# Two places where weights are split, one order inside the w_out units, and a last unit in three PSUM tiles

## The chip, the cores and the metric

The kernel runs on one core of a Trainium2 chip. The metric is the device time of one execution in microseconds (us). The kernel before took 1111.39 us, the median of three runs (1110.79 to 1111.77).

## The reference

Sigmoid attention, then a gated two-layer product, all in float32. With B = 8 batches, H = 12 heads, S = 448 positions and D = 64:

```
scores = q @ k.T / sqrt(64) - log(448)
attn   = 1 / (1 + exp(-scores))
x      = (attn @ v), heads side by side: 3584 x 768
h      = x @ w_in                      # 768 x 2048
g      = h * clip(h + 3, 0, 6) / 6
out    = g @ w_out                     # 2048 x 768
```

w_in and w_out arrive as 64-bit floats, which the kernel takes apart itself into 32-bit ones (`decode`: one ScalarE instruction and six VectorE ones for each piece).

## The kernel before

The engines are TensorE (PE), VectorE (DVE), ScalarE (ACT), GpSimd (POOL) and SyncE (SP), which issues every transfer. Each engine works through its instructions in the order in which the code was written (`manual_schedule`), so the order is set by hand: lists of steps (`on`), slots (`at_slot`) and units (`at_unit`) say in which step a piece of side work is written down.

Three stages follow each other on PE.

Attention has 168 steps. Step s writes the scores of step s, a sigmoid (`a`, L194), then the side work listed for s, then the product with v of step s - 2 (`av`). A finished pair is copied by ACT (`y`, L219) and added by DVE (`xr`, L220), which frees one of two PSUM buffers. Side work is the decoding of w_in, and for the first pair of batches four sums of x (`x_sums`, L234 to L240) and seven splits (`x_split`). A split turns a float32 tile into a high and a low part for PE: ACT casts (L69), DVE subtracts (L71).

The product stage, x times w_in, has 112 slots of 18 matmuls each (L345), seven products (M1 to M7) of Strassen's kind for each quarter. Slot n loads the weights of slot n + 5 into one of three staging buffers, casts those of slot n + 3 and subtracts those of n + 2; the subtraction frees the buffer. The first two w_out tiles (`w2_load`, `w2_split` for M1, h = 0 and 1) go through the same three buffers, in slots 90 to 97. A buffer is handed on in the order in which the code frees it.

The w_out stage has 56 units of 36 matmuls (L630): seven phases (M1, M2, M6, M7, M5, M4, M3), in each four pairs p, for each two halves h. Unit n needs `gx` of n, the split of a tile g of 128 x 1792, and the three w_out tiles of its phase and half. In unit n the code loads g of n + 4 (`g_load`), in two phases a second part of n + 3 (`g_load2`), sums the parts of n + 2 (`g_sum`) and splits g of n + 2. Between the cast and the subtraction of that split stands the unit's listed work (`plan`): decoding w_out pieces (`w2_unit`, L50 to L63), four sums of its quarters (`w2_sums`, three on DVE, L531 to L533, the fourth on POOL, L534), storing them (`w2_store`, L539), loading and splitting the next phase's tiles (L458, L69, L71). Two units make one PSUM tile `po` of three banks, which `post2` turns into a sum kept (`s`) or an output (`o`, L567); the last unit does it for its three parts one after another (L567, and the transfers of L594). A w_out tile with h = 1 can be cast only when PE is done with the unit before the phase, since its three buffers are all in use.

Of the kernel before, what the change touches and what calls it, by code (L numbers as in the profile page):

```python
# [8 lines left out]
F32 = mybir.dt.float32  # L9
# [7 lines left out]
B, H, S, D = 8, 12, 448, 64  # L17
DM, DF = 768, 2048
P = 128
# [5 lines left out]
EC = DM // P // 2  # L25
# [12 lines left out]
M1, M2, M3, M4, M5, M6, M7 = range(7)  # L38
A11, A12, A21, A22, S1, S2, S3, S4 = range(8)
# [27 lines left out]
def split(nc, hi, lo, a):  # L67

    nc.scalar.copy(hi, a)  # L69
    yield  # L70
    nc.vector.tensor_tensor(out=lo, in0=a, in1=hi.bitcast(F32), op=ALU.subtract)  # L71
    yield
# [20 lines left out]
def tile_kernel(ctx: ExitStack, tc: tile.TileContext, qk, vP, wi, wo, outT):  # L93
# [45 lines left out]
    def ring(name, shape, dtype):  # L139
        return dw.tile(shape, dtype, tag="ring", name=name, bufs=5)  # L140
# [10 lines left out]
    events, later, plan = {}, {}, {}  # L151
# [4 lines left out]
    def at_slot(n, f, *a):  # L156
        later.setdefault(n, []).append((f, a))

    def at_unit(n, f, *a):
        plan.setdefault(n, []).append((f, a))  # L160

    def over(when, steps, gen):
        for n in steps:
            when(n, next, gen, None)
# [78 lines left out]
    def x_split(p, k):  # L243
        x = xt[k].tile([P, 2, KC, S], F32R, tag="x", name=f"x_{p}_{k}")
        xts[p, k] = x
        yield from split(nc, x[:, 0], x[:, 1], xr[p].pop(k))
# [19 lines left out]
    def w2_unit(k, h, ec, held):  # L266

        st = staging(f"wo_{k}_{h}_{ec}", [P, FC * P, 2], I32)
        nc.sync.dma_start(out=st, in_=wo[k, h, :, ec * FC * P : (ec + 1) * FC * P])
        yield  # L270
        if ec == 0:
            held[k, h] = ring(f"w2_{k}_{h}", [P, EC, FC * P], F32)
        yield from decode(nc, st, held[k, h][:, ec])
        if ec == EC - 1 and k in (A11, A12):
            yield
            yield
            nc.sync.dma_start(out=dw2[k, h], in_=held.pop((k, h)))
# [5 lines left out]
    for u in range(4 * EC):  # L283
        kh, ec = divmod(u, EC)
# [19 lines left out]
    end0 = 2 * LB + LAG  # L304
    over(on, range(end0 + 1, end0 + 5), x_sums(nc.vector, 0))
    for i, k in enumerate((B11, B22, B21, T3, T1, T2, T4)):
        over(on, (end0 + 6 + 2 * i, end0 + 7 + 2 * i), x_split(0, k))
    for n in range(LA):
        on(NS - 10 + n, w1_load, n)
        over(on, (NS - 3 + n, NS - 2 + n), w1_split(n))  # L310
# [112 lines left out]
    units = [(i, p, h) for i in PHASES for p in range(NPR) for h in range(2)]  # L423
# [7 lines left out]
    def g_load(n):  # L431
        if n < len(units):
            i, p, h = units[n]
            first, _ = PARTS.get(MOVING[i], (MOVING[i], None))
            gr[n] = gset[n % 3].tile([P, FC, S], F32, tag="gr", name=f"gr_{n}")
            nc.sync.dma_start(out=gr[n], in_=gd[p, first, h])

    def g_load2(n):
        if n < len(units) and MOVING[units[n][0]] in PARTS:
            i, p, h = units[n]  # L440
            gs[n] = [ring(f"gr_{n}_{k}", [P, 2, S], F32) for k in range(2)]
            for k in range(2):
                nc.sync.dma_start(out=gs[n][k], in_=gd[p, PARTS[MOVING[i]][1], h][:, 2 * k : 2 * k + 2])

    def g_sum(n):
        for k, o in enumerate(gs.pop(n, ())):
            part = gr[n][:, 2 * k : 2 * k + 2]
            nc.vector.tensor_tensor(out=part, in0=part, in1=o, op=ALU.subtract)  # L448

    def g_split(n):  # L450
        gx[n] = gset[n % 3].tile([P, 2, FC, S], F32R, tag="gx", name=f"gx_{n}")
        yield from split(nc, gx[n][:, 0], gx[n][:, 1], gr.pop(n))
# [7 lines left out]
    def w2_split(i, h):  # L460
        st, gens = w2s.pop((i, h)), []
        for ec in range(EC):
            w = xs.tile(
                [P, 2, FC, P], F32R, tag="xT" if h else "xraw", name=f"w2_{i}_{h}_{ec}", bufs=3 if h else 5
            )
            flat = w.rearrange("p t c e -> p t (c e)")
            w2[i, h, ec] = w
            gens.append(split(nc, flat[:, 0], flat[:, 1], st[:, ec]))
        for _ in range(2):
            for g in gens:  # L470
                next(g)
            yield
# [12 lines left out]
    end = len(seq)  # L485
    for n in range(LA, end):
        over(at_slot, (n - LA, n - LA + 1), w1_split(n))
    for h in range(2):
        at_slot(end - 22 + h, w2_load, M1, h)
        over(at_slot, (end - 18 + 2 * h, end - 17 + 2 * h), w2_split(M1, h))  # L490

    def xt_close(*ks):
        for k in ks:
# [12 lines left out]
    for n, (i, q) in enumerate(seq):  # L506
# [10 lines left out]
    po_pool = ctx.enter_context(  # L517
        tc.tile_pool(name="ps_o", bufs=2, space=bass.MemoryType.PSUM, reuse_waits="tile")
    )
# [21 lines left out]
    def w2_direct(i, h):  # L541
        w2s[i, h] = made[h].pop(WEIGHT[i])

    for h, n in ((0, 0), (1, 9)):
        for e in range(2 * EC):
            k, ec = divmod(e, EC)
            u = n + e
            over(at_unit, [max(0, u - 1), u, u + 1, u + 1, u + 1, u + 1], w2_unit(A21 + k, h, ec, held))
        at_unit(n + 4, w2_reload, h)
        at_unit(n + 2 * EC + (h == 0), w2_sums, h)  # L550
        at_unit(n + 2 * EC + 2, w2_store, h, *((S1, A22, S3, S2) if h == 0 else (S1, A22, S3)))
        at_unit(n + 2 * EC + 3, w2_store, h, S4)
    for k, i in enumerate(PHASES[1:]):
        n = 8 * (k + 1)
        for h in range(2):
# [7 lines left out]
    po, so = {}, {}  # L563
    SIXTH = 1.0 / 6.0

    def stt(out, ps_in, other):
        nc.vector.scalar_tensor_tensor(out=out, in0=ps_in, scalar=SIXTH, in1=other, op0=ALU.mult, op1=ALU.add)  # L567
# [4 lines left out]
    def out_tile(i, p):  # L572
        return acc_ctx[0].tile([P, EC, S], F32, tag="o", name=f"o_{i}_{p}", bufs=2)

    def kept(i, p):
        return acc_ctx[0].tile([P, EC, S], F32, tag="s", name=f"s_{i}_{p}", bufs=2 * NPR)

    def post2(i, p, n):
        t = po.pop(p)[:, :, :S]
        if i == M1:  # L580
            so[p] = kept(i, p)
            nc.scalar.mul(so[p], t, SIXTH)
        elif i == M6:
            stt(so[p], t, so[p])
        elif i == M7:
            so["u3", p] = kept(i, p)
            stt(so["u3", p], t, so[p])
        else:
            eh, k, other = {M2: (0, 0, p), M5: (1, 1, ("u3", p)), M4: (1, 0, ("u3", p)), M3: (0, 1, p)}[i]
            o = out_tile(i, p)  # L590
            if n == len(units) - 1:
                for ec in range(EC):
                    stt(o[:, ec], t[:, ec], so[other][:, ec])
                    nc.sync.dma_start(out=outT[2 * p + k, eh * EC + ec], in_=o[:, ec])  # L594
                return
            stt(o, t, so[other])
            if i == M5:
                stt(so[p], t, so[p])
            at_unit(n + 1, put, p, eh, k, o)

    for n, (i, p, h) in enumerate(units):
        if n == 0:
            for _ in range(2):
                for f, a in later.pop(min(later)):
                    f(*a)
        elif n == 1:
            while later:
                for f, a in later.pop(min(later)):
                    f(*a)
            tmp_ctx.close()  # L610
            acc_ctx.append(ctx.enter_context(tc.tile_pool(name="acc", bufs=1, side="right", reuse_waits="tile")))
        g_load(n + 4)
        g_load2(n + 3)
        low = None
        if n + 2 < len(units):
            g_sum(n + 2)
            low = g_split(n + 2)
            next(low)
        for f, a in plan.pop(n, []):
            f(*a)  # L620
        if low is not None:
            next(low)
        if h == 0:
            po[p] = po_pool.tile([P, EC, 512], F32, tag="po", name=f"po_{i}_{p}")
        x = gx.pop(n)
        for ec in range(EC):
            w = w2[i, h, ec]
            for c in range(FC):
                for wk, xk in ((0, 0), (0, 1), (1, 0)):
                    nc.tensor.matmul(  # L630
                        po[p][:, ec, :S],
                        w[:, wk, c],
                        x[:, xk, c],
                        start=h == 0 and c == 0 and xk == 0 and wk == 0,
                        stop=h == 1 and c == FC - 1 and wk == 1,
                    )
        if h == 1:
            post2(i, p, n)
# [34 lines left out]
```

## Time and profile before

| | us |
|---|---|
| median of three runs | 1111.39 |
| the profiled execution | 1116.47 |
| its span | 1114.7 |
| PE busy | 1091.8 |
| attention, first matmul to the first product matmul | 4.4 to 263.7 |
| product stage | 263.7 to 687.2 |
| w_out stage | 687.2 to 1110.1 |

A row of the timeline has the start in us from the span's start, the duration, the engine, the line, the operation with out<-in, and in brackets the idle time before it and what ended it. "x18" says that the row merges 18 instructions. "SPq" rows are transfers being issued, not their landing. The chain of waits merges instructions the same way: start, length, engine, tile, line. A wait is given as engine and tile <- what it waited for: us in total, times, longest.

### The profile page before, as it was taken

To read this page: it belongs to the slowest core of one execution; us is meant where nothing else is said; L and a number is where in the kernel's file an instruction comes from. 1 tells how busy PE (TensorE), PEld (TensorE's weight loads), DVE (VectorE), ACT (ScalarE), POOL (GpSimd) and SP (SyncE) were. 2 spreads that over 40 slices of the span, in tenths; PEclk is the share of its full clock that TensorE was granted. 3 is DMA by queue.
4 is the path that set the end of the run, shared out by engine and by line. 5 is a ranking of instruction groups with operands and counts; after the bars stand their busy time and mean duration, and the time that the engine had idled before them with its cause. 6 is when DMAs were issued, how large, how long until landed. Compare 5 with 4: busy or idle time off the path is not lost.

```text
span 1114.7 us, 16569 instructions
## 1 busy us (share of the span) xinstructions
PE 1091.8 (98%) x6720; PEld 865.4 (78%) x6720; DVE 744.0 (67%) x710; ACT 560.7 (50%) x612; POOL 177.2 (16%) x84
## 2 busy tenths in 40 slices
PE   8999999999999999999999899999999999989998
PEld 3333633336999999999999799999889999979997
DVE  3579747644677986898687456887863447776541
ACT  6889888876446554644565444443322212222320
POOL 0214120000252352244121112110000000000000
PEclk9999999999999999999999899999999999999999
DMA  8876998966665886687666687959775357889641
GB/s 313 303 285 250 360 356 317 309 238 206 208 220 179 295 269 204 200 288 237 200 198 223 220 257 239 338 191 393 268 270 189 132 194 260 291 298 314 238 143 50
DMA packets 81484, 277.13 MB, mean 249 GB/s; under 512 B 7936, under 2 KB 22272, under 8 KB 81408
## 3 DMA queue, kind: packets, MB, share of 16 engines
q1 hardware_dynamic: 81408, 276.07, 71.2%
q8 instruction: 53, 0.87, 0.3%
q14 instruction: 23, 0.19, 0.0%
HBM read 189.92 MB, written 86.11 MB: 248 GB/s over the span
## 4 chain that ended last, share of the span: by engine, by line
PE 84%; DVE 9%; ACT 3%; DMA 3%; issue 2%; SPq 0%; DVEq 0%; ACTq 0%
PE po L630 28%; PE A L345 21%; PE D L345 10%; PE sc L192 10%; PE pv L209 10%; PE B L345 5%; DVE gr L448 2%; ACT gx L69 2%; DVE gx L71 1%; DVE w L71 1%; DMA ws<-dw 1%; DVE x L71 1%; DMA w2s<-dw 1%; DVE o L567 1%; ACT w L69 0%
## 5 line engine op out<-in xcount | busy, mean ns | idle before, releaser
L630 PE MATMUL po<-gx,w 128*128 128x448 f32 x2016 | 416.9, 369 | 6.0 <-ACT w L69 3.4
L630 PEld LDWEIGHTS po<-gx,w 128*128 128x128 f32 x2016 | 379.4, 188 | 43.3 <-ACT w L69 4.2
L345 PE MATMUL A<-x,w 128*128 128x448 f32 x1152 | 245.7, 371 | 4.9 <-ACT u L370 4.8
L345 PEld LDWEIGHTS A<-x,w 128*128 128x128 f32 x1152 | 218.2, 190 | 27.7 <-ACT u L370 5.7
L69 ACT CAST gx<-gr 128x1792 fp32r<-128x1792 f32 x56 | 94.7, 1694 | 238.6 <-PE po L630 137.0
L192 PE MATMUL sc<-qk 64*64 64x448 f32 x1344 | 191.5, 542 | 5.0 <-DMA qk<-qk 4.4
L209 PE MATMUL pv<-a,v 64*64 64x448 f32 x1344 | 190.4, 537 | 2.3 <-DVE xr L220 2.0
L194 ACT ACTIVATE a<-sc,bias_s 128x896 f32<-128x896 f32 x168 | 169.0, 1010 | 46.5 <-PE sc L192 43.5
L71 DVE TENSOR_TENSOR w<-ws,w 128x768 fp32r<-128x768 f32 x112 | 154.1, 1385 | 32.2 <-ACT w L69 31.9
L71 DVE TENSOR_TENSOR gx<-gr,gx 128x1792 fp32r<-128x1792 f32 x56 | 113.2, 2022 | 70.5 <-ACT gx L69 70.5
L192 PEld LDWEIGHTS sc<-qk 64*64 64x64 f32 x1344 | 63.9, 134 | 80.5 <-issue 62.9
L209 PEld LDWEIGHTS pv<-a,v 64*64 64x64 f32 x1344 | 64.3, 133 | 77.0 <-issue 69.8
L345 PE MATMUL D<-x,w 128*128 128x448 f32 x576 | 123.9, 368 | 0.0
L345 PEld LDWEIGHTS D<-x,w 128*128 128x128 f32 x576 | 108.2, 188 | 10.5
L69 ACT CAST w<-ws 128x768 fp32r<-128x768 f32 x112 | 93.0, 831 | 33.6 <-DMA ws<-dw 33.6
L379 POOL TENSOR_TENSOR gT<-g,g 128x896 f32<-128x896 f32 x16 | 42.9, 2680 | 290.5 <-DVE g L356 290.5
L220 DVE TENSOR_TENSOR xr<-pv,y 128x448 f32<-128x448 f32 x48 | 29.8, 621 | 54.6 <-ACT y L219 54.6
L345 PE MATMUL B<-x,w 128*128 128x448 f32 x288 | 62.0, 368 | 0.0
L365 ACT ACTIVATE g<-cD,bias 128x896 f32<-128x896 f32 x32 | 33.5, 1047 | 49.1 <-DVE cD L374 25.2
L345 PEld LDWEIGHTS B<-x,w 128*128 128x128 f32 x288 | 54.1, 188 | 5.3
L370 ACT COPY u<-A 128x896 f32<-128x896 f32 x32 | 29.0, 906 | 52.9 <-PE A L345 52.7
L374 DVE TENSOR_TENSOR cD<-D,u 128x896 f32<-128x896 f32 x32 | 34.8, 1088 | 24.9 <-ACT u L370 15.7
(59 smaller groups left out, 737.4 us busy)
## 6 DMA issues: line engine op xcount, KB each, us to landing
gr<-gd SPq DMA_DIRECT2D x56, 896.0 KB, 4.8
ws<-dw SPq DMA_DIRECT2D x112, 384.0 KB, 3.9
gd<-g SPq DMA_DIRECT2D x64, 448.0 KB, 4.8
qk<-qk SPq DMA_DIRECT2D x48, 448.0 KB, 6.6
gd<-gT SPq DMA_DIRECT2D x32, 448.0 KB, 5.3
gr<-gd SPq DMA_DIRECT2D x32, 448.0 KB, 6.1
wi<-wi SPq DMA_DIRECT2D x16, 768.0 KB, 7.8
wo<-wo SPq DMA_DIRECT2D x24, 512.0 KB, 6.4
```

The costliest lines, as they stand in the source:

```text
L69: nc.scalar.copy(hi, a)
L71: nc.vector.tensor_tensor(out=lo, in0=a, in1=hi.bitcast(F32), op=ALU.subtract)
L192: nc.tensor.matmul(out, k[halves[r], at_k], q[halves[r]], start=True, stop=True)
L194: nc.scalar.activation(a, sc[:, :, :S], AF.Sigmoid, bias=bias_s, scale=scale)
L209: nc.tensor.matmul(pv[p][halves[j], r, :S], v, a[halves[r], int(r != j) if c is None else j], start=first, stop=last)
L220: nc.vector.tensor_tensor(out=xr[b, u][:, k], in0=pv[p][:, 1, :S], in1=y, op=ALU.add)
L345: nc.tensor.matmul(t[:, j, :S], w[:, wk, j, kc], x[:, xk, kc], start=i in (M1, M2, M5) and m == 0, stop=m == 3 * KC - 1, skip_group_check= ...
L365: nc.scalar.activation(r, h, AF.Relu, bias=bias_3, scale=1.0)
L370: nc.scalar.copy(acc[key, q], acc["A", q][:, :, :S])
L374: nc.vector.tensor_tensor(out=c, in0=acc[name, q][:, :, :S], in1=acc[key, q], op=ALU.add)
L379: nc.gpsimd.tensor_tensor(out=t3, in0=quad[q, B22], in1=quad[q, B12], op=ALU.subtract)
L630: nc.tensor.matmul(po[p][:, ec, :S], w[:, wk, c], x[:, xk, c], start=h == 0 and c == 0 and xk == 0 and wk == 0, stop=h == 1 and c == FC - ...
```

## The change

It has four parts. The seven splits of the first pair's x start one step earlier and are six steps apart instead of two. The second of the first two w_out tiles is loaded seven slots after the first, and each is split two slots after its load. In the w_out stage, the load of a second g part stands ahead of the g load, a unit's listed work stands ahead of g's sum and split, and the split is no longer in two pieces; the second half's w_out decoding begins at unit 8 instead of 9, and both halves' sums and stores stand a unit earlier in their turn. The last two units use three PSUM tiles of one bank each.

```
     for i, k in enumerate((B11, B22, B21, T3, T1, T2, T4)):
-        over(on, (end0 + 6 + 2 * i, end0 + 7 + 2 * i), x_split(0, k))
+        over(on, (end0 + 5 + 6 * i, end0 + 6 + 6 * i), x_split(0, k))
...
     for h in range(2):
-        at_slot(end - 22 + h, w2_load, M1, h)
-        over(at_slot, (end - 18 + 2 * h, end - 17 + 2 * h), w2_split(M1, h))
+        at_slot(end - 22 + 7 * h, w2_load, M1, h)
+        over(at_slot, (end - 20 + 7 * h, end - 19 + 7 * h), w2_split(M1, h))
...
-    for h, n in ((0, 0), (1, 9)):
+    for h, n in ((0, 0), (1, 8)):
...
-        at_unit(n + 2 * EC + (h == 0), w2_sums, h)
-        at_unit(n + 2 * EC + 2, w2_store, h, *((S1, A22, S3, S2) if h == 0 else (S1, A22, S3)))
-        at_unit(n + 2 * EC + 3, w2_store, h, S4)
+        at_unit(n + 2 * EC, w2_sums, h)
+        at_unit(n + 2 * EC + 1, w2_store, h, *((S1, A22, S3, S2) if h == 0 else (S1, A22, S3)))
+        at_unit(n + 2 * EC + 2, w2_store, h, S4)
...
-                    stt(o[:, ec], t[:, ec], so[other][:, ec])
+                    stt(o[:, ec], t[ec], so[other][:, ec])
...
+        g_load2(n + 3)
         g_load(n + 4)
-        g_load2(n + 3)
-        low = None
+        for f, a in plan.pop(n, []):
+            f(*a)
         if n + 2 < len(units):
             g_sum(n + 2)
-            low = g_split(n + 2)
-            next(low)
-        for f, a in plan.pop(n, []):
-            f(*a)
-        if low is not None:
-            next(low)
-        if h == 0:
+            for _ in g_split(n + 2):
+                pass
+        if h == 0 and n == len(units) - 2:
+            po[p] = [po_pool.tile([P, 512], F32, tag="pl" if ec < 2 else "po", name=f"pl_{ec}")[:, :S] for ec in range(EC)]
+        elif h == 0:
             po[p] = po_pool.tile([P, EC, 512], F32, tag="po", name=f"po_{i}_{p}")
```

What this does to the order of instructions is shown at three places. The first is SP in slots 90 to 93 of the product stage: `ws_94` is the weight load of slot 94, `w2s_0_0` and `w2s_0_1` are the two w_out tiles, `gd` rows store g. Before:

```order
L294 DMA ws_94_5379<-dw1_1_70 128x768
L458 DMA w2s_0_0_5405<-dw2_0_0_73 128x1536
L294 DMA ws_95_5408<-dw1_1_70 128x768
L458 DMA w2s_0_1_5433<-dw2_0_1_74 128x1536
L294 DMA ws_96_5436<-dw1_2_71 128x768
L361 DMA gd_3_2_0_127<-g2_12_5377 128x896
L294 DMA ws_97_5466<-dw1_1_70 128x768
```

And now:

```order
L294 DMA ws_94_5379<-dw1_1_70 128x768
L458 DMA w2s_0_0_5405<-dw2_0_0_73 128x1536
L294 DMA ws_95_5408<-dw1_1_70 128x768
L294 DMA ws_96_5434<-dw1_2_71 128x768
L361 DMA gd_3_2_0_127<-g2_12_5377 128x896
L294 DMA ws_97_5470<-dw1_1_70 128x768
```

The second w_out tile has left its place ahead of `ws_96`; it now stands behind `ws_101`.

The second place is ACT at the beginning of the w_out stage: `gx_2` is the cast of g for unit 2, and `w2_2_0` from `wo_2_0_0` the first instruction of decoding the first w_out piece. Before:

```order
L69 CAST gx_1_6059<-gr_1_5971 128x1792
L69 CAST gx_2_6071<-gr_2_6050 128x1792
L50 ACTIVATE w2_2_0_6075<-wo_2_0_0_6073 128x512
L69 CAST gx_3_6126<-gr_3_6052 128x1792
L50 ACTIVATE w2_2_0_6075<-wo_2_0_1_6077 128x512
```

And now:

```order
L69 CAST gx_1_6059<-gr_1_5971 128x1792
L50 ACTIVATE w2_2_0_6073<-wo_2_0_0_6071 128x512
L69 CAST gx_2_6077<-gr_2_6050 128x1792
L50 ACTIVATE w2_2_0_6073<-wo_2_0_1_6075 128x512
L69 CAST gx_3_6135<-gr_3_6052 128x1792
```

The cast of each unit's g has moved behind one decoding instruction, which waits for its w_out transfer.

The third place is SP in units 6 to 8: `w2s_1_1` is the second phase's w_out tile for h = 1, which unit 9 uses, the `dw2` rows of L539 store the sums, `gr_11` is the load of g for unit 11. Before:

```order
L458 DMA w2s_1_0_6395<-dw2_1_0_75 128x1536
L436 DMA gr_11_6435<-gd_1_1_1_102 128x1792
L458 DMA w2s_1_1_6453<-dw2_1_1_76 128x1536
L436 DMA gr_12_6494<-gd_2_1_0_113 128x1792
L539 DMA dw2_4_0_79<-w2S1_0_6439 128x1536
L539 DMA dw2_3_0_77<-w2_3_0_6237 128x1536
L539 DMA dw2_6_0_83<-w2_2_0_6075 128x1536
L539 DMA dw2_5_0_81<-w2r_0_0_6293 128x1536
L269 DMA wo_2_1_0_6502<-wo 128x1024
```

And now:

```order
L458 DMA w2s_1_0_6398<-dw2_1_0_75 128x1536
L436 DMA gr_11_6440<-gd_1_1_1_102 128x1792
L539 DMA dw2_4_0_79<-w2S1_0_6393 128x1536
L539 DMA dw2_3_0_77<-w2_3_0_6235 128x1536
L539 DMA dw2_6_0_83<-w2_2_0_6073 128x1536
L539 DMA dw2_5_0_81<-w2r_0_0_6291 128x1536
L269 DMA wo_2_1_0_6446<-wo 128x1024
L458 DMA w2s_1_1_6457<-dw2_1_1_76 128x1536
L436 DMA gr_12_6500<-gd_2_1_0_113 128x1792
```

The stores and the w_out load have moved ahead of the load of `w2s_1_1`, and all of them stand behind `gr_11`, whose buffer is freed by the subtraction of g for unit 8.

More of the change, by code (lines that the diff above doesn't have):

```diff
@@ L578, in post2 @@
     def post2(i, p, n):
-        t = po.pop(p)[:, :, :S]
+        t = po.pop(p)
+        if n < len(units) - 1:
+            t = t[:, :, :S]
         if i == M1:
@@ L630, in tile_kernel @@
                     nc.tensor.matmul(
-                        po[p][:, ec, :S],
+                        po[p][ec] if n > len(units) - 3 else po[p][:, ec, :S],
                         w[:, wk, c],
```

## The prediction

> **What bounds the kernel now.** I read the page first, then the waits of TensorE (PE), then the chain and the timeline at each place where PE waits.
>
> ```profile
> span 1114.7 us, 16569 instructions
> PE 1091.8 (98%) x6720; PEld 865.4 (78%) x6720; DVE 744.0 (67%) x710; ACT 560.7 (50%) x612; POOL 177.2 (16%) x84
> GB/s 313 303 285 250 360 356 317 309 238 206 208 220 179 295 269 204 200 288 237 200 198 223 220 257 239 338 191 393 268 270 189 132 194 260 291 298 314 238 143 50
> ...
> PE A L345 <- ACT u L370: 4.8, 1, 4.8
> ```
>
> PE works 98% of the span: only 1114.7 - 1091.8 = 22.9 us are open, and the change moves no matmul. A gain can come only from these waits, from the slower matmuls behind them, and from the tail. The longest row of waits stands above; each place is taken in turn. The profiled execution took 1116.47 us (span 1114.7 and 1.8 around it); the median shown is 1111.39. I sum in the profile's microseconds and take the result off the median, as if both had the same waits.
>
> **Attention: x splits six steps apart.** The scores of steps 30, 45, 60 and 66, two VectorE (DVE) rows with the wait that they end, and a quiet window of before:
>
> ```profile
> 49.48 0.93 PE L192 MATMUL sc<-qk 64*64 64x448 f32 x8
> 72.03 0.93 PE L192 MATMUL sc<-qk 64*64 64x448 f32 x8
> 97.73 0.93 PE L192 MATMUL sc<-qk 64*64 64x448 f32 x8
> 107.71 0.93 PE L192 MATMUL sc<-qk 64*64 64x448 f32 x8
> ...
> 91.41 1.55 DVE L71 TENSOR_TENSOR x<-xr,x 128x1344 fp32r<-128x1344 f32 x1
> 94.75 0.62 DVE L220 TENSOR_TENSOR xr<-pv,y 128x448 f32<-128x448 f32 x1
> 95.42 0.98 PE L209 MATMUL pv<-a,v 64*64 64x448 f32 x8 [1.46 <-DVE xr L220]
> ...
> 40.00:60.00 20.00, 20.00 (x216) 7.98 (x212) 12.52 (x18) 16.13 (x20) 3.92 (x4) 1.00 0.88 321
> ```
>
> From 49.48 to 72.03 fifteen steps take 22.55 us, 1.503 each, so step 60 is 97.73 - 72.03 - 22.55 = 3.15 late and step 66 4.1: that is the loss. The wait at 95.42 ends with the xr at 94.75, the end of an unbroken DVE queue. The change takes one split (1.55, the one at 91.41) from ahead of it, so this xr ends near 93.9. Without any slip PE would want it at 95.42 - 3.15 = 92.3; 1.6 stay lost. The sums ahead of it aren't moved. Behind it DVE gets one split per 9 us, and the second slip (1.0, step 66) goes. ScalarE (ACT) then has a 1.3 us cast on top of 16.13 busy of 20 us (the window's fourth number); where the cast falls beside a y copy I allow 0.5 in all. Gain 4.1 - 2.1 = 2.0; bounds 1.0 (ACT costs 1.5) and 3.0 (nothing left but 1.1).
>
> **Product stage: the second w_out tile seven slots later.** Three staging buffers carry the w_in weights. Two w_out tiles held two of them, and the rest came one at a time.
>
> ```profile
> 602.48 3.72 PE B L345 x18
> 629.86 6.41 PE A L345 x18
> 636.27 3.65 PE B L345 x18
> ...
> 608.22 0.32 SPq L458 DMA_DIRECT2D w2s<-dw  x1
> 610.97 0.95 DVE L71 TENSOR_TENSOR w<-ws,w 128x768 fp32r<-128x768 f32 x1
> 615.79 0.83 ACT L69 CAST w<-ws 128x768 fp32r<-128x768 f32 x1 [3.60 <-DMA ws<-dw]
> 622.46 0.83 ACT L69 CAST w<-ws 128x768 fp32r<-128x768 f32 x1 [5.03 <-DMA ws<-dw]
> 624.20 1.89 DVE L71 TENSOR_TENSOR w<-w2s,w 128x512 fp32r<-128x512 f32 x3
> ```
>
> Weights come every 6.67 us (615.79, 622.46) where a slot takes 3.72. From one B to the next, seven slots, 33.79 us pass where 7 x 3.72 = 26.04 would: 7.75 lost, 2.7 of it the 18 matmuls of 6.41 us at a lower clock. Afterwards, with the second tile gone, 608.22 carries a weight transfer, which at the row's 3.6 to 3.9 lands at 612; the buffer freed at 611.9 brings the next at 615.8; the first tile's three subtractions now stand behind that one and free the third buffer at 611.9 + 1.9 = 613.8. Two buffers turn round every 6.67, or 3.3 per weight, under 3.72. Casts and copies lie inside ACT's idle 3.60 and 5.03. The second tile meets the same seven-slot pattern later. Nothing is late next, so 7.75 go. One thing is given back: behind the wait a slot takes 3.65, before it 3.72, and 14 slots follow to the stage's end; without the wait I keep 3.72 there: 1.0. Gain 6.7; bounds 5.0 and 7.75.
>
> **w_out stage: w_out ahead of g.** A unit is 36 matmuls, 7.39 us (103.50 / 14 below). Two old losses go.
>
> ```profile
> 687.35 103.50 PE po L630 x504
> 997.51 112.52 PE po L630 x540
> ...
> 806.62 5.19 DVE L71 TENSOR_TENSOR w<-w2s,w 128x512 fp32r<-128x512 f32 x3
> 806.83 3.82 POOL L534 TENSOR_TENSOR w2r<-w2r,w2r 128x1536 f32<-128x1536 f32 x1 [60.93 <-DVE w2r L533]
> 807.35 2.73 PE L630 MATMUL po<-gx,w 128*128 128x448 f32 x12 [1.32 <-DVE w L71]
> 811.25 18.95 PE L630 MATMUL po<-gx,w 128*128 128x448 f32 x91 [1.17 <-DVE w L71]
> ```
>
> Unit 16 was due at 687.2 + 16 x 7.393 = 805.5, its third matmul, the first to read a weight's subtraction, at 805.9; it came at 807.35, and the third of the second tile 1.4 late again: 3.0 lost. From there, 811.25, to unit 41 at 997.51 are 22 matmuls and 24 units, 181.9 us; 186.3 passed, and the last 15 units took 112.52 instead of 111.0: 5.9 lost at units 40 and 41, where the weight casts stood behind g's sum and cast. Now they stand ahead, and g 42 still has a unit's time. Together 8.9 go.
>
> New waits come. First, unit 2. ACT decodes w_out tile 0 ahead of the cast of g 2:
>
> ```profile
> 689.51 3.27 ACT L69 CAST gx<-gr 128x1792 fp32r<-128x1792 f32 x2
> 694.16 2.02 DVE L71 TENSOR_TENSOR gx<-gr,gx 128x1792 fp32r<-128x1792 f32 x1
> 700.07 0.66 ACT L50 ACTIVATE w<-wo 128x512 f32<-128x512 f32 x1 [7.29 <-DMA wo<-wo]
> ```
>
> The second cast of the 689.51 pair is g 2. It now waits with ACT for the transfer that lands at 700.0: cast 700.7 to 702.4, subtraction to 704.4. Unit 2 is due at 702.0 and its second matmul reads the subtraction: 2.2 lost (1.0 to 2.6).
>
> Second, unit 9, which needs w_out tile 1 of the second phase. SyncE (SP) issued its load a unit ahead of the stores; now it goes behind a g load, four stores of 768 KB and a w_out load. That g load waits for the subtraction of g 8, which now stands behind the sums:
>
> ```profile
> 728.02 0.42 DVE L52 TENSOR_SCALAR w<-w 128x512 f32<-128x512 f32 x1
> 730.86 0.69 DVE L63 TENSOR_TENSOR w<-w,wo 128x512 f32<-128x512 f32 x1
> 736.58 1.75 DVE L531 TENSOR_TENSOR w2S<-w,w 128x1536 f32<-128x1536 f32 x1
> 741.83 5.22 DVE L71 TENSOR_TENSOR w<-w2s,w 128x512 fp32r<-128x512 f32 x3
> ...
> 749.06 0.32 SPq L436 DMA_DIRECT2D gr<-gd  x1
> 752.40 0.61 SPq L269 DMA_DIRECT2D wo<-wo  x1
> 764.23 0.66 ACT L50 ACTIVATE w<-wo 128x512 f32<-128x512 f32 x1 [8.63 <-DMA wo<-wo]
> ```
>
> The last of six decodes ended at 731.5; DVE now starts on them at 704.4, behind g 2, not at 700.7, so it ends near 735. Sums 5.25 (736.58 to 741.83) and g 8 (2.0): the g load goes out at 742. The same g load, four stores and w_out load took 749.06 to 764.2, 15.1 us; tile 1 of 768 KB adds 2.0 at the 393 GB/s of the page's best slice: landed 759.1, cast and first subtraction ready by 760. Due: 753.7 + 2.2 = 755.9. Lost 3.9; if all 5.4 MB ran at 393 GB/s (13.7 us, and 2 to start), 2.7. After the last old wait the 15 units lost 1.5 to the clock, so I add 1.5; bounds 2.7 and 8.0. [...]
>
> Third, unit 16 again. Sums and GpSimd's (POOL) subtraction come a unit earlier, with g 16's subtraction now between them and the weights.
>
> ```profile
> 694.33 3.85 POOL L379 TENSOR_TENSOR gT<-g,g 128x896 f32<-128x896 f32 x1 [16.77 <-DVE g L356]
> 698.26 2.13 POOL L381 TENSOR_TENSOR gT<-gT,g 128x896 f32<-128x896 f32 x1
> ```
>
> The first took 1.7 longer than its like: it sat out the DVE subtraction begun at 694.16. And one of the three subtractions at 806.62 sat out POOL. From unit 14's start DVE now has an output step (1.6, as the tail's three parts), a decode (3.5: 728.0 to 731.5), the sums (5.25) and g 16 (1.9); then POOL's 3.6 (2.13 x 1536 / 896) and 0.5 for the weight's subtraction: 16.3. Its matmul is due 2 x 7.39 + 0.4 = 15.2 after that start: 1.1 lost (0 to 2.5). [...]
>
> Stage: -8.9 + 2.2 + 5.4 + 1.1 = -0.2: nearly all is given back (-5.2 to +4.2).
>
> **Tail.**
>
> ```profile
> 1110.06 1.69 DVE L567 SCALAR_TENSOR_TENSOR o<-po,s 128x448 f32<-128x448 f32 x3 [13.22 <-PE po L630]
> 1110.71 1.39 SPq L594 DMA_DIRECT2D outT<-o  x3
> ```
>
> Three results waited for the last matmul. With three PSUM tiles two run under the 24 and 12 matmuls left (4.9 and 2.5 us); one of 0.6 remains: gain 1.1.
>
> **Sum.** 2.0 + 6.7 + 0.2 + 1.1 = 10.0, so 1111.4 - 10.0 = 1101.4. The best ends add to a gain of 17, the worst to 2.9.
>
> **Rivals.** (a) The stores move at the best slice's rate and POOL doesn't block: 2.2 + 2.7 lost in the w_out stage instead of 8.7, 1097.6. For it, the slice of 393 GB/s; against it, the same transfers took 15.1 us. 0.12. (b) The product stage falls into the 3.65 slot from its start: 112 x 0.07 = 7.8 more, 1093.6. Rows show both paces, and that a wait separates them; which one a fresh start takes they don't. 0.07. (c) The change doesn't do what it says in the product stage: the first tile's transfer or subtractions come late and a weight still waits there; the 6.7 stay, and the second tile, seven slots on, meets a lesser wait of some 2: 1110. Against it, the first tile was issued before the second (608.22), over 16 us ahead of its subtraction at 624.20. 0.07. (d) Slower: the store burst at units 7 to 9. It decides from a landing of tile 1 at 768, 9 later than reckoned: 5.4 MB at 228 GB/s, and many slices of the page show less. Then unit 9 loses 12.9, the clock 2.7 and the loads behind it some 2: 1101.4 - 5.4 + 17.6 = 1113.6; a landing at 771 gives 1116.6. Against it, those slices had little to move. 0.05.
>
> **How the numbers follow.** The forecast's case has 0.69. Range 1096.5 to 1106.5: it holds that case with unit 9 at 8.0 and attention at its worst, and (a); (b), (c) and (d), 0.19, are outside. A measurement of this kernel tells about 0.2%, 2.2 us. Faster: 0.88; same, (c): 0.07; slower, (d): 0.05.
>
> **What would show it.** Right: no wait of PE on ACT's u near 617 to 630, slots of 3.72 to the stage's end; PE waits at unit 2 (702, 2 us, ACT behind the w_out transfer), at unit 9 on the weight cast (about 4 us) and little at unit 16; none at units 40 and 41; a last output of one tile. Wrong: a product stage at 3.65, ACT's casts delaying scores by more than 1.5 us, or tile 1 landing before 756 or after 765.

## The result, and the profile after

The changed kernel takes 1099.03 us (median of 4 runs, 1098.51 to 1100.41); the kernel before, timed beside it, 1111.09 (1110.59 to 1111.77). The ratio is 0.9895, with a 95% interval of 0.9881 to 0.9909: 11.7 us faster by the ratio, 12.1 by the medians. The forecast was 1101.4, a gain of 10.0. The profiled execution took 1098.91 us, like the median. The head of its page and its waits of PE (in all, how many, the longest):

```profile
span 1097.1 us, 16580 instructions
PE 1082.8 (99%) x6720; PEld 859.1 (78%) x6720; DVE 747.4 (68%) x710; ACT 562.5 (51%) x612; POOL 180.9 (16%) x84
...
PE po L631 <- ACT w L69: 2.7, 1, 2.7
PE po L631 <- DVE gx L71: 1.6, 1, 1.6
PE po L631 <- DVE w L71: 1.2, 1, 1.2
```

The 4.8 us wait on `u` is gone from the product stage, and so are the waits of units 40 and 41. Three waits stand in the w_out stage now, at units 2, 9 and 16. Stage by stage (from the first matmul of a stage to the first of the next, then to the start of the last matmul, then to the end of the span), with the runs of the next section below for comparison; "opening" is what the third attention step lost while TensorE was still at half pace, which differs between executions (a 64x448 matmul took 951 ns ahead of the opening and 536 ns behind it; the step began at 7.4 us in the kernel before and in the changed one, and the clock opened at 7.29 in the first and at 9.52 in the second, where the records of the granted clock begin, with 1.0):

| us | attention | opening in it | product | w_out | tail |
|---|---|---|---|---|---|
| before | 259.27 | 0 | 423.48 | 422.47 | 5.04 |
| after | 258.10 | 1.07 | 408.69 | 422.17 | 3.82 |
| x splits only | 258.42 | 1.36 | 416.66 | 422.64 | 5.04 |
| first tiles only | 259.82 | 0.57 | 408.69 | 422.96 | 5.04 |
| tail only | 260.93 | 1.29 | 417.60 | 422.56 | 3.81 |
| unit order only | 259.47 | 0.16 | 417.83 | 424.22 | 5.04 |
| after, g first | 258.22 | 1.12 | 408.69 | 416.21 | 3.81 |
| after, early load | 257.33 | 0.27 | 408.69 | 423.64 | 3.82 |
| after, fourth sum on DVE | 257.94 | 0.89 | 408.69 | 420.96 | 3.81 |
| g first and tile 1 | 257.79 | 0.77 | 408.69 | 415.05 | 3.81 |
| x sums spread | 257.84 | 0.29 | 408.68 | 415.05 | 3.82 |

**Attention.** The step that was late after the x splits still waits for an xr, but for less:

```profile
94.47 0.62 DVE L220 TENSOR_TENSOR xr<-pv,y 128x448 f32<-128x448 f32 x1
95.14 0.98 PE L209 MATMUL pv<-a,v 64*64 64x448 f32 x8 [0.59 <-DVE xr L220]
```

It was 1.46. Without the opening the stage takes 257.03 in place of 259.27.

**Product stage.** The chain at the place where PE used to stand:

```profile
609.26 10.95 PE A L345 x54
620.20 3.64 PE B L345 x18
```

Three slots in 10.95 and the next in 3.64, with no wait between them. The whole stage is 112 slots of 3.65. That pace is not the one that the profile of before had up to its wait (3.72).

**Unit 2.** ACT, DVE and PE around it:

```profile
683.80 0.66 ACT L50 ACTIVATE w<-wo 128x512 f32<-128x512 f32 x1 [8.69 <-DMA wo<-wo]
684.37 1.68 ACT L69 CAST gx<-gr 128x1792 fp32r<-128x1792 f32 x1
...
686.08 2.03 DVE L71 TENSOR_TENSOR gx<-gr,gx 128x1792 fp32r<-128x1792 f32 x1 [7.90 <-ACT gx L69]
...
688.16 14.12 PE L631 MATMUL po<-gx,w 128*128 128x448 f32 x60 [1.59 <-DVE gx L71]
```

The decode waited 8.69 us for its transfer with the cast of g 2 behind it, and PE then waited 1.59 for the subtraction that follows from it.

**Unit 9.** SyncE's g load and the load of tile 1, ACT's cast of that tile, and PE:

```profile
726.52 0.32 SPq L436 DMA_DIRECT2D gr<-gd  x1
...
730.10 0.71 SPq L458 DMA_DIRECT2D w2s<-dw  x1
...
743.52 1.66 ACT L69 CAST w<-w2s 128x512 fp32r<-128x512 f32 x3 [1.16 <-DMA w2s<-dw]
...
744.20 6.13 PE L631 MATMUL po<-gx,w 128*128 128x448 f32 x27 [2.71 <-ACT w L69]
```

From the g load to the landing of tile 1 (743.5), behind four stores and a w_out load, 17.0 us pass; 17.1 were forecast.

**Unit 16.** DVE's subtraction of g 16, GpSimd's sum, the weights' subtractions, PE:

```profile
792.13 2.02 DVE L71 TENSOR_TENSOR gx<-gr,gx 128x1792 fp32r<-128x1792 f32 x1
...
792.35 5.16 POOL L534 TENSOR_TENSOR w2r<-w2r,w2r 128x1536 f32<-128x1536 f32 x1 [62.47 <-DVE w2r L533]
794.07 5.20 DVE L71 TENSOR_TENSOR w<-w2s,w 128x512 fp32r<-128x512 f32 x3
...
798.12 5.20 PE L631 MATMUL po<-gx,w 128*128 128x448 f32 x24 [1.18 <-DVE w L71]
```

GpSimd's sum begins 0.22 us behind the subtraction of g 16, and takes 5.16 where it took 3.82 before. Of the three weight subtractions the first lasts 3.99 us, to 0.55 behind the end of GpSimd's sum (798.06 and 797.51), and the others 0.68 each; PE waits for the first.

**Tail.** DVE at the end:

```profile
1088.76 0.63 DVE L567 SCALAR_TENSOR_TENSOR o<-pl,s 128x448 f32<-128x448 f32 x1 [8.30 <-PE pl L631]
...
1093.69 0.62 DVE L567 SCALAR_TENSOR_TENSOR o<-pl,s 128x448 f32<-128x448 f32 x1 [1.84 <-PE pl L631]
```

Two of three results are made under the matmuls; one of 0.62 is left.

### The profile page after: what moved, and what is told of

It is laid out like the page before. It is cut to its first block, busy times and chain, and to the rows that moved or that the text cites. A ratio compares the mean times of both kernels' runs of the same rounds, so it can differ in the third digit from the quotient of the medians.

```text
span 1097.1 us, 16580 instructions
## 1 busy us (share of the span) xinstructions
PE 1082.8 (99%) x6720; PEld 859.1 (78%) x6720; DVE 747.4 (68%) x710; ACT 562.5 (51%) x612; POOL 180.9 (16%) x84
## 4 chain that ended last, share of the span: by engine, by line
PE 91%; DVE 5%; DMA 2%; ACT 1%; issue 1%; SPq 0%; ACTq 0%; DVEq 0%
PE po L631 31%; PE A L345 21%; PE sc L192 11%; PE D L345 11%; PE pv L209 10%; PE B L345 5%; PE pl L631 1%; DMA w2s<-dw 1%; DVE gx L71 1%; DMA wo<-wo 1%; ACT gx L69 0%; DVE w L71 0%; ACT a L194 0%; DMA qk<-qk 0%; DVE w L532 0%
## 5 line engine op out<-in xcount | busy, mean ns | idle before, releaser
L631 PE MATMUL po<-gx,w 128*128 128x448 f32 x1944 | 402.2, 369 | 5.6 <-ACT w L69 2.7
L631 PEld LDWEIGHTS po<-gx,w 128*128 128x128 f32 x1944 | 365.8, 188 | 41.7 <-ACT w L69 3.1
L345 PE MATMUL A<-x,w 128*128 128x448 f32 x1152 | 238.9, 365 | 0.0
L192 PE MATMUL sc<-qk 64*64 64x448 f32 x1344 | 160.3, 544 | 4.3 <-DMA qk<-qk 4.3
L209 PE MATMUL pv<-a,v 64*64 64x448 f32 x1344 | 159.0, 537 | 1.0 <-DVE xr L220 0.6
L192 PEld LDWEIGHTS sc<-qk 64*64 64x64 f32 x1344 | 51.2, 134 | 81.8 <-issue 58.9
L209 PEld LDWEIGHTS pv<-a,v 64*64 64x64 f32 x1344 | 51.3, 134 | 78.7 <-issue 74.0
```

The costliest lines, as they stand in the source:

```text
L192: nc.tensor.matmul(out, k[halves[r], at_k], q[halves[r]], start=True, stop=True)
L209: nc.tensor.matmul(pv[p][halves[j], r, :S], v, a[halves[r], int(r != j) if c is None else j], start=first, stop=last)
L345: nc.tensor.matmul(t[:, j, :S], w[:, wk, j, kc], x[:, xk, kc], start=i in (M1, M2, M5) and m == 0, stop=m == 3 * KC - 1, skip_group_check= ...
L631: nc.tensor.matmul(po[p][ec] if n > len(units) - 3 else po[p][:, ec, :S], w[:, wk, c], x[:, xk, c], start=h == 0 and c == 0 and xk == 0 an ...
```

## The experiments

Two theories stood against each other on the product stage. Theory A: the pace of a slot differs between executions, and the timed executions of before run at 3.65 for the most part; the profiled one, 5 us above their median, didn't. Theory B: before always runs at 3.72, and something in the change makes it 3.65. The w_out stage had a theory of its own: the order's gain of 8.9 is lost again at units 2, 9 and 16, each for the reason in the prediction.

**The kernel before once more** (no edit).

> The kernel before, unchanged. Its profiled execution of 1116.47 us had product slots of 3.72 us up to the wait near 617 and of 3.65 behind it; the changed kernel's had 3.65 throughout. Theory A (the pace of a slot differs from execution to execution, and the timed executions of before ran at 3.65 already): ratio 1.000 within 0.2%, and a profile with slots of 3.65 from the start of the stage, 1109 to 1112 us, the wait on the weights still there and some 0.5 us longer. Theory B (the kernel before always runs at 3.72 and the change brings the 3.65): the profile shows 3.72 again, while its time is near 1111 for some other reason.

Measured: 1111.44 against 1110.77, ratio 1.0006 (0.9986 to 1.0026). The profiled execution took 1819.56 us at a granted clock of 0.557, and tells nothing of the pace. The timed ones do: of the 64 other executions of this kernel in the experiments, ten took 1116.0 to 1118.2 us and the rest 1108.0 to 1113.8. The profiled 1116.47 of before lies among the ten. 94 slots at 3.72 in place of 3.65 are 6.8 us, the distance between the two groups. None of the 64 has a profile, so that this pace is what parts the groups is worked out from that distance and not seen.

**Each part alone, on the kernel before.** The x splits:

```diff
-        over(on, (end0 + 6 + 2 * i, end0 + 7 + 2 * i), x_split(0, k))
+        over(on, (end0 + 5 + 6 * i, end0 + 6 + 6 * i), x_split(0, k))
```

> The kernel before with the x splits alone six steps apart. Theory A: a gain of 2.0 us (0.9982), bounds 1.0 and 3.0; slips of the attention steps fall from about 4.1 to 2.1 us. Theory B, if this part is what sets the pace of the product slots: some 2 + 6.8, that is 1102.5 us. Nothing for both: the slips move, but an equal sum is lost later.

Measured: 1108.87, ratio 0.9971 (0.9957 to 0.9985). By the medians 1.9 gained; the 1102.5 of theory B isn't seen. In the table the attention without its opening falls from 259.27 to 257.06: 2.2.

The first two w_out tiles:

```diff
-        at_slot(end - 22 + h, w2_load, M1, h)
-        over(at_slot, (end - 18 + 2 * h, end - 17 + 2 * h), w2_split(M1, h))
+        at_slot(end - 22 + 7 * h, w2_load, M1, h)
+        over(at_slot, (end - 20 + 7 * h, end - 19 + 7 * h), w2_split(M1, h))
```

> The kernel before with the first two w_out tiles alone fetched seven slots apart. Theory A (both at 3.65): the wait and the half clock go, 7.75 + 0.5 = 8.2 us gained, 1103 us. Theory as in the prediction (3.72 kept in the slots behind): 6.7 gained, 1104.5. Theory B with this part setting the pace: 7.75 + 6.8, 1096.7.

Measured: 1102.33, ratio 0.9917 (0.9897 to 0.9936): 8.4 gained by the medians, 9.2 by the ratio. Theory A had 8.2, the prediction's term was 6.7, theory B 14.6. The product stage takes 408.69, the same as in the changed kernel.

The last unit in three PSUM tiles:

```diff
-                    stt(o[:, ec], t[:, ec], so[other][:, ec])
+                    stt(o[:, ec], t[ec], so[other][:, ec])
...
+        if h == 0 and n == len(units) - 2:
+            po[p] = [po_pool.tile([P, 512], F32, tag="pl" if ec < 2 else "po", name=f"pl_{ec}")[:, :S] for ec in range(EC)]
```

> The kernel before with the last unit in three PSUM tiles alone. Prediction's term: 1.1 us gained (0.9990), the span from the last matmul to the end 1.2 shorter. Rival: the last transfer sets the end alone, and nothing is gained.

Measured: 1110.02, ratio 0.9985 (0.9969 to 1.0). The time alone can't tell so little; the tail of the span can, 3.81 for 5.04. This run says more about the pace, because up to the last unit it is the kernel before. Its chain around the old wait:

```profile
601.13 3.66 PE D L345 x18
...
625.38 6.56 PE A L345 x18
631.93 3.65 PE B L345 x18
```

Slots of 3.65 already ahead of the wait: the product stage as before has it does run at this pace. It takes 417.60 so, 416.66 in the run with the x splits; against 408.69 the first tiles are worth 8.0 to 8.9. Theory B would need each of these separate edits to bring the pace, and two thirds more gain from the first tiles than was measured: it falls.

The new order inside the units:

```diff
-    for h, n in ((0, 0), (1, 9)):
+    for h, n in ((0, 0), (1, 8)):
...
+        for f, a in plan.pop(n, []):
+            f(*a)
         if n + 2 < len(units):
             g_sum(n + 2)
-            low = g_split(n + 2)
-            next(low)
-        for f, a in plan.pop(n, []):
-            f(*a)
-        if low is not None:
-            next(low)
+            for _ in g_split(n + 2):
+                pass
```

> The kernel before with the new order inside the w_out units alone (w_out ahead of g, sums and stores a unit earlier, second half from unit 8). The prediction's sum for this stage: 8.9 lost at units 16, 40 and 41 goes, 2.2 at unit 2, 5.4 at unit 9 and 1.1 at unit 16 come: 0.2 gained, and waits of PE at units 2, 9 and 16. From the changed kernel's trace: 3.7 at units 1 and 2 with half a clock, 3.3 at unit 9, 1.5 at unit 16, 0.4 gained. Rival: the order is a plain gain of 8.9 and the losses of the changed kernel have another cause: 1102.

Measured: 1112.65 against 1111.43, ratio 1.0003 (0.9981 to 1.0026). The waits of PE in the w_out stage:

```profile
PE po L627 <- ACT w L69: 4.4, 1, 4.4
...
PE po L627 <- DVE gx L71: 1.6, 1, 1.6
PE po L627 <- DVE w L71: 1.4, 2, 1.2
```

The same three places as in the changed kernel. The stage takes 424.22 for 422.47, 2.1 more than in the changed kernel: this part alone gains nothing, and the rival's 8.9 is refuted. Its chain around the old wait of the product stage is of use as well:

```profile
596.04 3.65 PE B L345 x18
...
623.19 6.54 PE A L345 x18
629.72 3.72 PE B L345 x18
```

Here the pace goes from 3.65 to 3.72 at the wait; in the profile of before it went the other way.

**The pace, drawn again on purpose.** The changed kernel with some weights made late:

```diff
-        over(at_slot, (n - LA, n - LA + 1), w1_split(n))
+        over(at_slot, (n, n) if n % 14 == 0 else (n - LA, n - LA + 1), w1_split(n))
```

> The changed kernel with every 14th w_in weight (14, 28, ... 98) cast and subtracted only in its own slot, so that PE waits there 1 to 3 us. Theory A (a slot's pace, 3.65 or 3.72, is drawn anew at each interruption of PE and holds to the next): of eight stretches some run at 3.72, most at 3.65. Rival (the pace is drawn once, at the start of an execution or of the stage): all eight have one pace. Price: 7 waits, 10 to 20 us, and half clocks behind the longer ones.

Measured: 1132.73 in one run, 33.7 above the changed kernel where 10 to 20 were priced. PE's rows around the second and the third wait (start, busy; a slot's pace is the distance between starts, the busy time holds the end of its last matmul too):

```profile
354.43 3.81 PE L345 MATMUL D<-x,w 128*128 128x448 f32 x18
358.07 11.11 PE L345 MATMUL A<-x,w 128*128 128x448 f32 x54
372.21 6.80 PE L345 MATMUL B<-x,w 128*128 128x448 f32 x18 [3.03 <-ACT w L69]
378.85 3.88 PE L345 MATMUL D<-x,w 128*128 128x448 f32 x18
382.57 3.88 PE L345 MATMUL A<-x,w 128*128 128x448 f32 x18
...
429.18 5.73 PE L345 MATMUL B<-x,w 128*128 128x448 f32 x18 [1.82 <-ACT w L69]
434.75 3.88 PE L345 MATMUL D<-x,w 128*128 128x448 f32 x18
438.47 3.88 PE L345 MATMUL A<-x,w 128*128 128x448 f32 x18
```

Starts 3.64 apart ahead of 372.21, 3.72 behind it and behind 429.18 too, then 3.65 again in the four stretches behind the fourth wait and later ones: two of eight stretches at 3.72. The rival's one pace for all eight falls: the pace changed at an interruption, and held between two. What decides it stays open.

**g first where no weight is split.** The changed kernel, with g's sum and whole split ahead of the listed work in all units but 7, 8, 15, 16, and so on:

```diff
+        g_first = n == 0 or n % 8 not in (7, 0)
+        for part in range(2):
+            if (part == 0) == g_first:
+                if n + 2 < len(units):
+                    g_sum(n + 2)
+                    for _ in g_split(n + 2):
+                        pass
+            else:
+                for f, a in plan.pop(n, []):
+                    f(*a)
```

> The changed kernel with g ahead of w_out again in every unit but those in which a weight is split (7, 8, 15, 16, ...), unit 0 among those with g first. Theory: the wait at unit 2 (1.85, and 1.7 of half clock behind it) came from the cast of g 2 standing behind the decode; it goes, and the wait at unit 9 falls by some 1 since the sums start earlier: 4 us gained, 1095, and no new wait at units 40 and 41. Rival: unit 9 is bound by when its transfer lands; what unit 2 gives is lost there again: 1097.5 to 1099.

Measured: 1093.04 (5 runs, 1091.75 to 1093.40), ratio to before 0.9816 (0.9788 to 0.9844): 6.0 under the changed kernel by the medians and by the w_out stage (416.21 for 422.17), where 4 was expected. What is left of PE's waits in the w_out stage:

```profile
PE po L635 <- ACT w L69: 0.9, 1, 0.9
PE po L635 <- DVE w L71: 0.7, 1, 0.7
```

The wait at unit 2 is gone and unit 9's fell from 2.7 to 0.9. Unit 16's went as well, which I had not counted: the subtraction of g 16 now comes ahead of the sums, and nothing of it stands between GpSimd's sum and the weights. Units 40 and 41 stay clean. So the rival, that unit 9 would take it all, falls.

**The load of tile 1 a unit earlier**, on the changed kernel:

```diff
-                at_unit(n - 2 + h, w2_load, i, h)
+                at_unit(n - 2 + (h if k else 0), w2_load, i, h)
```

> The changed kernel with the load of w_out tile 1 of the second phase one unit earlier, ahead of the stores on SyncE. Theory (it is late for standing behind the stores): tile 1 lands near 724 instead of 743.5; what is left of the 3.3 us wait at unit 9 is the cast behind a decode that waits for its own w_out transfer, 1.5 to 2; 1.3 to 1.8 us gained. Rival (the DVE queue, not the transfer, makes unit 9 late): 3.3 stay.

Measured: 1098.69, ratio to before 0.9870 (0.9838 to 0.9902); no gain on the changed kernel that the times can tell. SyncE, ACT and PE:

```profile
715.58 2.13 SPq L458 DMA_DIRECT2D w2s<-dw  x2
...
741.33 0.66 ACT L50 ACTIVATE w<-wo 128x512 f32<-128x512 f32 x1 [7.82 <-DMA wo<-wo]
741.89 1.64 ACT L69 CAST w<-w2s 128x512 fp32r<-128x512 f32 x3
...
742.54 7.76 PE L631 MATMUL po<-gx,w 128*128 128x448 f32 x23 [2.97 <-ACT w L69]
```

The tile lands at 724.3, yet its cast comes at 741.89: it stands behind a decode that waited 7.82 us for a w_out transfer, the one in the queue right ahead of the old place, which is itself behind the four stores. Counted from the stage's first matmul (671.12 in the changed kernel, 670.46 here), PE goes on at 72.1 in place of 73.1: one microsecond of the 1.3 to 1.8 expected. The wait is as long as before only because PE came to it earlier. Behind it came 6.8 us at half clock, and the stage is 1.5 longer than the changed kernel's (423.64 for 422.17).

**The fourth sum on VectorE**, in the second half of the changed kernel:

```diff
-        nc.gpsimd.tensor_tensor(out=a[A12], in0=a[A12], in1=a[A11], op=ALU.subtract)
+        engine = nc.vector if h else nc.gpsimd
+        engine.tensor_tensor(out=a[A12], in0=a[A12], in1=a[A11], op=ALU.subtract)
```

> The changed kernel with the fourth sum of the second half (one subtraction) on VectorE instead of GpSimd. Theory (GpSimd and VectorE shut each other out): the weight subtractions of 5.2 us beside it become 3 x 0.63, DVE gets 1.8 more to do, and the wait of 1.45 at unit 16 goes: 1.4 us gained. Rival (the queue of DVE is simply too long there): the 1.8 more make the wait at unit 16 longer, 3 us, and nothing is gained.

Measured: 1098.35, ratio to before 0.9871 (0.9833 to 0.9908). DVE at unit 16:

```profile
792.36 1.76 DVE L535 TENSOR_TENSOR w2r<-w2r,w2r 128x1536 f32<-128x1536 f32 x1
...
795.97 1.89 DVE L71 TENSOR_TENSOR w<-w2s,w 128x512 fp32r<-128x512 f32 x3
```

DVE has one operation more and is done sooner: 1.89 for the three subtractions that took 5.20 beside GpSimd. The loss at unit 16 (1.45 in the changed kernel) is gone, and the stage is 1.2 shorter. The rival, a queue that is simply too long, falls.

**Both at units 8 and 9**, on the kernel with g first: the early load, and the fourth sum of the first half on VectorE (`engine = nc.gpsimd if h else nc.vector`).

> The kernel of the run with g first, with two more edits against the wait of 2.5 us that it still has at units 8 and 9: tile 1 of the second phase is loaded a unit earlier, ahead of the stores, and the fourth sum of the first half runs on VectorE. Theory: 0.7 of the 2.5 is a subtraction that shares its time with GpSimd, 0.9 and the rest the late transfer; both go, PE waits nowhere in the w_out stage, 2.4 us gained against 1093.0: 1090.6. Rival (as in the run with the early load alone: the decode ahead of the cast waits for its own transfer): 1 to 2 stay, 1092.

Measured: 1091.45 (5 runs, 1090.86 to 1091.87), ratio to before 0.9821 (0.9796 to 0.9846); 1.6 under the run with g first by the medians (the kernel before took 1111.43 beside that run and 1111.15 beside this one), 1.2 by the stage, of 2.4 expected. Unit 9 waits no more; which of the two edits did that wasn't tried. Unit 8 still does, on DVE:

```profile
729.14 1.76 DVE L535 TENSOR_TENSOR w2r<-w2r,w2r 128x1536 f32<-128x1536 f32 x1
...
730.82 1.89 DVE L71 TENSOR_TENSOR w<-w2s,w 128x512 fp32r<-128x512 f32 x3
731.55 13.61 PE L636 MATMUL po<-gx,w 128*128 128x448 f32 x65 [1.04 <-DVE w L71]
```

The sum that was put on DVE now stands itself ahead of the weights. It is the best version tried, 19.7 us under the kernel before.

**The x sums spread too**, on the kernel of the run just above:

```diff
-    over(on, range(end0 + 1, end0 + 5), x_sums(nc.vector, 0))
+    over(on, range(end0 + 1, end0 + 9, 2), x_sums(nc.vector, 0))
...
-        over(on, (end0 + 5 + 6 * i, end0 + 6 + 6 * i), x_split(0, k))
+        over(on, (end0 + 9 + 6 * i, end0 + 10 + 6 * i), x_split(0, k))
```

> The kernel of the run before this one with the first pair's four x sums two steps apart too, and the splits four steps later. Theory (what the attention still loses, 1.1 at step 59 and some 0.9 around it, is DVE's queue with the sums in it): about 1.5 to 2 us gained, 1089. Rival (it comes from ScalarE's casts or from GpSimd beside DVE): the slips of steps 55 to 64 stay or move, 0.

Measured: 1091.48 against 1091.45: nothing, and without the opening the attention is 0.5 longer. The theory falls. The waits moved into one place, where 0.6 became 1.7:

```profile
86.41 1.31 POOL L79 TENSOR_TENSOR wS<-wS,wA 128x384 f32<-128x384 f32 x1
...
86.89 1.25 DVE L53 TENSOR_SCALAR wA<-wA 128x768 int32<-128x768 int32 x1
...
94.46 0.98 PE L209 MATMUL pv<-a,v 64*64 64x448 f32 x8 [1.71 <-DVE xr L220]
...
95.44 0.56 DVE L53 TENSOR_SCALAR wA<-wA 128x768 int32<-128x768 int32 x1
```

The same DVE operation takes 1.25 beside GpSimd's w_in sums and 0.56 without them. Those sums run until 89.0, beside the queue that DVE works off ahead of the late xr, and may be what is left of the loss here; that they are was not tried.

## Why the prediction was right, and where it was off

**The direction and the range** held: a gain of 12.1 by the medians for 10.0 forecast. One of its own signs of being wrong came true all the same, "a product stage at 3.65".

**Attention, 2.0:** right in size and cause. 2.2 without the opening, 1.9 by the time of the part alone. The 1.6 that were to stay lost at the late xr are 1.12 in step 59 and 0.6 in the steps ahead of it. What the prediction didn't have is the opening of the clock, 0 to 1.4 us from execution to execution, up to two thirds of this term.

**Product stage, 6.7:** the mechanism was right, since PE waits for no weight any more; the size was off, and this is the step that failed. I gave 1.0 back for 14 slots that "without the wait I keep" at 3.72, and I took the result off the median "as if both had the same waits". Neither holds. The two paces are no property of a wait that is there or isn't. The spread of the timed runs and the profiles of three kernels that share before's code around this wait say that most executions of before run at 3.65 from the start; so nothing is given back. The wait itself cost 8.0 to 8.9 in the stages compared above, and 8.4 by the time of the part alone, for 7.75 in the profile of before; that shorter slots leave the weights less time may be why, but isn't shown, since the wait differs by 1.1 us between two runs of one pace (4.4 and 5.5 us). The comparison of profile with profile would have misled further: it gives 14.8 for this stage, of which 6.8 is the pace of one execution. The sign was in front of me: a profiled execution 5 us over a median whose runs lie within 1 us.

**Rival (b)**, the pace of 3.65 from the start, came true in the trace and not in the time. I priced it at 7.8 us and 1093.6, because I didn't see that most timed runs of before had, by their times, that pace already.

**w_out stage, -8.9 + 2.2 + 5.4 + 1.1 = -0.2 lost:** right to 0.2 in the sum: 8.7 over 56 bare units before, 8.4 after, and nothing gained by the part alone. That the sum is so close is luck: unit 2 cost 1.5 more than forecast and unit 9 2.1 less. Place by place: the losses at 16 by the old cause and at 40 and 41 went. Unit 2: 3.7 lost in place of 2.2, of which 1.9 is wait and the rest the clock. Unit 9: 3.3 of wait and of what follows it, for 3.9 and 1.5 of clock; the lower bound of the 3.9 had 2 us for the burst to start, which no row shows by themselves (the three 224 KB transfers at the end of before took 2.0 us from issue to landing, their own time included), and the whole burst took 17.0 here. Unit 16: 1.45 for 1.1. So the waits were foreseen each at its place. Runs bear the reason out at unit 2 (with g first the wait is gone) and at unit 16 (with the sum on VectorE it is gone). At unit 9 tile 1 landed 72.4 us behind the stage's first matmul, for 71.9 forecast, but the early load shows a second hold that was not in the sum: the decode ahead of the cast, whose own w_out transfer also stands behind the stores. The clock was put behind the longer wait and came behind the shorter; the prediction had nothing that could have told which, and the runs below don't settle it.

Rival (a) needed a quicker burst and a GpSimd that doesn't block: the burst took 17.0 us for 17.1, and the run with the sum on VectorE shows the blocking (three subtractions in 5.20 us beside GpSimd, one of them alone 3.99, and 1.89 without it). Rival (c) needed a weight that PE still waits for, and there is none. Rival (d) needed a landing of tile 1 nine microseconds later than it was.

**Tail, 1.1:** 1.2, for the reason given.

## What to carry to other kernels

Hold the time of the profiled execution against the timed ones before summing from it: here it lay outside their spread because, as far as the runs show, one of its stages ran at another pace than theirs, and taking one profile from the other would have put 6.8 us of pace down to the change. When an order is changed to help two units of a long loop, change it in those units: the same order in the others made waits that ate the whole gain, and g first everywhere else brought 6 us more. And a load that is moved earlier gains little while the operation that uses it stands in line behind another one that waits for a transfer: here tile 1 landed at 724.3, its cast came at 741.89, behind a wait of 7.82 us, and PE went on one microsecond earlier.

## What the runs showed of the hardware

The same 18 matmuls of 448 columns, with nothing waiting, took 3.65 or 3.72 us (203 or 207 ns each), and kept to one until an interruption. Six of eight stretches in the run with the late weights ran at the first; 54 of 64 executions of before lie in the group that fits it.

Whether a wait cost clock was not told by its length. Windows of the changed kernel, with the granted clock behind the busy times (PEclk), after the wait of 1.59 us at unit 2 and after the one of 2.71 at unit 9, and of the run with the early load after its wait of 2.97 at unit 9:

```profile
688.70:692.20 3.50, 3.50 (x11) 3.10 (x10) 3.36 (x6) 0.82 (x1) 0.00 (x0) 0.51 0.86 305
...
743.00:751.00 8.00, 6.75 (x32) 5.87 (x33) 5.95 (x9) 5.45 (x6) 0.00 (x0) 1.00 0.74 275
```

```profile
686.00:700.00 14.00, 12.42 (x61) 11.19 (x61) 13.28 (x18) 6.24 (x7) 0.00 (x0) 1.00 0.72 258
742.20:749.10 6.90, 6.56 (x18) 5.70 (x19) 5.74 (x8) 5.18 (x6) 0.00 (x0) 0.53 0.56 195
```

The shorter wait was followed by 3.4 us at half clock and the longer by none; in the other run the wait at unit 2 (1.6 us as well) was followed by none, and that at unit 9 by 6.8. The stretches at half clock lasted 3.41 us or twice that. In the profiles of the kernels before and after, the clock's changes lie whole multiples of 3.413 us apart: the changed kernel's clock opened at 9.52, halved at 688.77, which is 199 of them later, and opened again at 692.18; before's opened at 7.29, halved at 628.51 (182 of them later), opened at 635.34 (2), halved at 997.15 (106) and opened at 1000.56 (1). It may matter, then, where on this grid a wait falls, but that alone doesn't settle it either: PE was busy for 1.79 us of the stretch that ended at 688.77, and the clock halved; it was busy for 1.52 us of the stretch that ended at 743.38, in the wait at unit 9, and the clock did not. What decides it was not shown.
